# Row loads behind the inverse's blocks, and two scalings moved, in a chunked RWKV-7 and GELU kernel

## The chip, the cores and the metric

The kernel runs on one core of a Trainium2 chip. Its time is the device time of one execution in microseconds. TensorE (PE in the profile) multiplies matrices into PSUM, VectorE (DVE), ScalarE (ACT) and GpSimd (POOL) work on tiles in SBUF, and SyncE (SP) only issues transfers, one after the other in the order of the program. Engines run beside each other and wait for each other by semaphores. An instruction that waits holds up everything behind it on its own engine.

## The reference

```python
for t in range(S):                       # B, H, S, D = 4, 8, 768, 40
    y[:, :, t] = einsum('bhd,bhde->bhe', r_t, state)
    Sa = einsum('bhde,bhe->bhd', state, a_t)
    state = state * w_t[:, :, None, :] - einsum('bhd,bhe->bhde', Sa, b_t)
    state = state + einsum('bhd,bhe->bhde', v_t, k_t)
x = y.transpose(0, 2, 1, 3).reshape(B * S, H * D)    # 3072 x 320
h = x @ w_in                                          # 320 x 2048
out = (0.5 * h * (1 + erf(h / sqrt(2)))) @ w_out      # 2048 x 320
```

A recurrence over 768 tokens in 32 independent heads, then a two-layer network with an exact GELU. All arithmetic is in float32.

## The kernel before, in words

The sequence is cut into 12 chunks of 64 tokens (`NCH`). Within a chunk the recurrence is written as matrix products over the 64 tokens, with running products of w in the place of the step by step decay. The correction by a and b needs the inverse of a triangular 64x64 matrix for each head, built from `N`, the masked product of b and a.

That inverse goes a long way round. `make_N` (L571) masks the product on VectorE and has SP write its two diagonal 32x32 blocks to DRAM (four transfers, L586). `start_inverse` (L622) loads them back into `Nb`, with one block in each partition (two transfers, L635), and `columns()` (L639) eliminates the 31 columns on GpSimd: per column a product (L643) and a sum (L645). `store_inverse` (L651) writes the result to DRAM from GpSimd's queue (L657), and `fetch_inverse` (L660) brings it back as `Tt` and `T2` over SP's queue (six transfers, L667 and L671). `turn_corner` (L678) transposes a part of it into `L` on VectorE (L680), from which `corner` (J on TensorE) and `joined` (J2, then L710) make the off-diagonal block.

The main loop (L1121 to L1208) works on three chunks at once. In the pass of chunk c it finishes c (`corner`, `make_X`, `joined`, `make_sa`, `make_M`, `make_QY`, `outputs`), does the later preparation of n = c + 1 (`make_A`, `fetch_inverse`, `make_av`, `make_RV`, `turn_corner`) and begins n2 = c + 2: its loads, its sums of log w, its N and the start of its inverse. Between these steps `fill()` puts one portion of the network of an earlier chunk (`mlp`, and from the fourth chunk on `seven`, a form of the second layer with seven products in place of eight) on TensorE, so that it always has something to do. The order of the instructions on every engine is written out by hand: it is the order of the program.

For n2 several arrays are loaded. `load_next` brings w and a, `load_r`, `load_v` and two calls of `fetch_pairs` bring r, v, b and k in pairs of tokens for transposition (`a_pairs`, `r_pairs`, `v_pairs`, each tile used for two arrays in turn). Beside these, v, b and k are loaded once more as plain rows: `load_VR` (L197, tile `VR`) and `load_kb` (L193, tiles `b_rows` and `k_rows`, two of each in turn), six transfers of 160 KB. The rows of b and k are scaled by the inverse running product of w (`part`, written in `sums`, L425): b on VectorE in `scale_b` (L463), k on GpSimd in `scale_k` (L470). The scaled rows are first needed by `make_QY`, a pass later; the rows of v by `make_av`, in the next pass.

So SP's queue in one pass holds, in this order and beginning in the middle: w, a, r, b in pairs, v, k in pairs, the ten small transfers of `xt` (L802, L805, the input of the network), the rows of v, b, k, the six fetches of the inverse of n, the four of N of n2, the two of Nb of n2, and the four stores of an earlier chunk's output.

In `seven`, VectorE forms sums and differences of blocks of `gt`, the activated hidden layer: L868 makes a difference `s2`, L869 makes another in place in `block(1, 0)`, which the second product of the third group (`m7`) reads; L875 makes the one in `block(0, 1)` that the first product of that group reads.

Of the kernel before, what the change touches and what calls it, by code (L numbers as in the profile page):

```python
# [19 lines left out]
def kernel(  # L20
# [46 lines left out]
    nc = tc.nc  # L67
# [125 lines left out]
    def load_kb(c):  # L193
        fetch(c, "b", b, nc.sync)
        fetch(c, "k", k, nc.sync)

    def load_VR(c):  # L197
        VR = turned_in.setdefault(c, {})["VR"] = VR_ring()
        for e in range(2):
            nc.sync.dma_start(out=VR[half(e)].rearrange("p g q m d -> p (g q m) d")[:, :, :D], in_=rows_of(v, c, e))  # L200
# [195 lines left out]
    def run(steps):  # L396
        for _ in steps:
            pass
# [60 lines left out]
    def scale_b(c):  # L459
        rwv, wp = decays[c]  # L460
        nb = padded[:, c % 2] if c < NB else b_rows[c % 2]
        to = nb[:, :, :, :D] if c < NB else rows(nb)
        nc.vector.scalar_tensor_tensor(to, raws.pop((c, "b")), -1.0, rwv, ALU.mult, ALU.mult)  # L463
        turned_in[c]["nb"] = nb

    def scale_k(c, eng=nc.gpsimd):
        rwv, _ = decays.pop(c)
        ks = turned_in[c]["ks"] = padded[:, 2 + c % 2] if c < NB else k_rows[c % 2]
        to = ks[:, :, :, :D] if c < NB else rows(ks)
        eng.tensor_tensor(to, raws.pop((c, "k")), rwv, ALU.mult)  # L470

    def scale(c):
        scale_b(c)
        scale_k(c)
# [147 lines left out]
    def start_inverse(c, eng, place=None):  # L622

        n = P // 2
        blk = blocks.pop(c).rearrange("j z n s t -> (j z n) s t")
        if place is None:
            Nb = work.tile([P, BL * BL], FP32, tag="Nb", name="Nb")
            W = work.tile([P, BL // 2 * BL], FP32, tag="W", name="W")
            tmp = work.tile([P, BL * BL // 7], FP32, tag="tmp", name="tmp")
        else:  # L630
            Nb, W, tmp = place
        Nb, W = (t.rearrange("p (s t) -> p s t", t=BL) for t in (Nb, W))
        eng.memset(W, 0.0)
        for par in range(2):
            nc.sync.dma_start(out=Nb[par * n:(par + 1) * n], in_=blk)  # L635
            eng.memset(W[par * n:(par + 1) * n].rearrange("p s t -> p (s t)")[:, par::BL + 2][:, :BL // 2], 1.0)
        inverses[c] = W

        def columns():  # L639
            for j in range(BL - 1):  # L640
                rows, rest = j // 2 + 1, BL - 1 - j
                t = tmp[:, :rows * rest].rearrange("p (s t) -> p s t", s=rows)
                eng.tensor_tensor(t, W[:, :rows, j:j + 1].to_broadcast([P, rows, rest]),  # L643
                                  Nb[:, j:j + 1, j + 1:].to_broadcast([P, rows, rest]), ALU.mult)
                eng.tensor_tensor(W[:, :rows, j + 1:], W[:, :rows, j + 1:], t, ALU.add)  # L645
                yield
        return columns()
# [49 lines left out]
    def joined(c):  # L697
        t = turned_in[c]
        Tt, T2 = inverses.pop(c)
        Js = t.pop("Js")  # L700
        F = flat(Tt)
        J = duo("J2")[:, :, :G * NP * BL].rearrange("p z (n t) -> p z n t", n=G * NP)
        for n in range(2 * G * NP):
            for q in range(2):
                if n % 2:
                    mm(J[lo[q], 1, n // 2], Js[lo[q], n // 2], T2[lo[q], n // 2])
                else:
                    mm(J[lo[q], 0, n // 2], Js[hi[q], n // 2], F[hi[q], n, BL:])
        for q, copy in ((0, nc.scalar.copy), (1, nc.vector.tensor_copy)):
            copy(F[lo[q], :, BL:].rearrange("p (n z) t -> p z n t", z=2), J[lo[q]])  # L710
        t["Tt"] = Tt
# [115 lines left out]
    def block(g, z):  # L827
        return gt[:, z * NF // 2:(z + 1) * NF // 2, g * P:(g + 1) * P]
# [15 lines left out]
    def seven(c, s1, s2):  # L844
        t1, t2, t4 = sums_of_w
        t3 = quarter(0, 1)
        os = [work.tile([P, 2, DM // 2], FP32, tag="os", name="os", bufs=2) for g in range(G)]
        c11, c12, c21, c22 = os[0][:, 0], os[0][:, 1], os[1][:, 0], os[1][:, 1]

        def products_of(*factors):  # L850
            po = duo("po")
            for n, (l_, r_) in enumerate(factors):
                for f in range(NF // 2):
                    nc.tensor.matmul(po[:, n, :DM // 2], l_[:, f], r_[:, f], start=f == 0, stop=f == NF // 2 - 1)  # L854
            return po[:, 0, :DM // 2], po[:, 1, :DM // 2]

        def add(to, one_, other):
            nc.vector.tensor_tensor(to, one_, other, ALU.add)  # L858

        def store(g):  # L860
            for e in range(2):
                row = (G * e + g) * S + c * C
                nc.sync.dma_start(out=out[row:row + C], in_=os[g][half(e)].rearrange("p z d -> p (z d)"))

        m1, m2 = products_of((block(0, 0), quarter(0, 0)), (block(0, 1), quarter(1, 0)))
        if s2 is None:
            s2 = SM_ring().rearrange("p e g n c -> p (e g n c)")[:, :NF * P // 2].rearrange("p (f t) -> p f t", t=P)
            nc.vector.tensor_tensor(s2, s1, block(0, 0), ALU.subtract)  # L868
        nc.vector.tensor_tensor(block(1, 0), block(0, 0), block(1, 0), ALU.subtract)  # L869
        nc.scalar.copy(c12, m1)  # L870
        nc.scalar.copy(c11, m2)
        add(c11, c11, c12)
        yield
        m5, m6 = products_of((s1, t1), (s2, t2))
        nc.vector.tensor_tensor(block(0, 1), block(0, 1), s2, ALU.subtract)  # L875
        nc.scalar.copy(c22, m5)  # L876
        add(c12, c12, m6)
        yield
        m3, m7 = products_of((block(0, 1), quarter(1, 1)), (block(1, 0), t3))
        add(c21, c12, m7)  # L880
        add(c12, c12, c22)
        add(c12, c12, m3)
        add(c22, c22, c21)
        store(0)
        yield
        m4, _ = products_of((block(1, 1), t4))
        add(c21, c21, m4)
        store(1)
        yield
# [231 lines left out]
    for c in range(2, NCH):  # L1121
        n, n2 = c + 1, c + 2
        more, more2 = n < NCH, n2 < NCH
        corner(c)
        make_X(c)
        if c == NS + 1:
            weight_sums(3)
        if c == 2:

            seconds(1, (14, 14), last=True)  # L1130
            fill()
            turn_b(n)
            make_N(n)
            run(start_inverse(n, nc.gpsimd))
            store_inverse(n, (nc.gpsimd,))
            load_r(n)
            load_v(n)
        else:
            fill()
        if more2:  # L1140
            load_next(n2)
        joined(c)
        if c == 2:
            pieces.reverse()
            seconds(2, last=True)
        fill()
        make_sa(c)
        make_saT(c)
        if c == 2:
            turn_r(n)  # L1150
            scale_k(n, nc.vector)
            fill()
            pieces.reverse()
            fill(2)
            turn_k(n)
        if more2:
            load_r(n2)
        if more2:
            turn_a(n2)
            fetch_pairs(n2, "b_turned", b, nc.sync, False, paired["a"])  # L1160
        fill()
        make_y2(c)
        make_M(c)
        if more:
            turn_v(n)
        if more2:
            load_v(n2)
            turn_r(n2)
            fetch_pairs(n2, "k_turned", k, nc.sync, False, paired["r"])
        fill()  # L1170
        if more2:
            logs(n2)
        make_QY(c)
        outputs(c)
        pieces.append(mlp(c))
        fill()
        if c == NS:
            weight_sums(0)
            weight_sums(1)
        if more:  # L1180
            make_A(n)
        if more2:
            load_VR(n2)
            load_kb(n2)
            sums(n2)
        if more:
            turn_state()
            fetch_inverse(n)
            make_av(n)
        if more2:  # L1190
            scale_a(n2)
            turn_b(n2)
        fill()
        if c == NS:
            weight_sums(2)
        if more:
            make_RV(n)
        if more2:
            make_N(n2)
            scale(n2)  # L1200
            run(start_inverse(n2, nc.gpsimd))
            store_inverse(n2, (nc.gpsimd,))
        if more:
            turn_corner(n)
        fill()
        if more2:
            turn_k(n2)
        fill()  # L1208
# [31 lines left out]
```

## Time and profile before

| | |
|---|---|
| median of 13 runs | 729.3 us (724.92 to 732.57) |
| the profiled execution | 725.5 us, its span 723.8 us |
| TensorE busy, matmuls | 664.3 us (92%) |
| VectorE, GpSimd, ScalarE busy | 383.5, 349.0, 213.6 us |
| one chunk on TensorE, undisturbed | 50.7 us (337.18 to 387.91) |
| inverse on GpSimd, one chunk | 29.9 us (342.04 to 371.98) to 32.9 us (500.30 to 533.21) |
| DMA queue of SP | 52.4% of 16 engines |

The span runs from the first to the last instruction of the profiled execution, and its times count from there. A line of the timeline gives start, duration, engine, line and operation, the tile written and the tiles read, the count, and in brackets the idle time of the engine before it and what ended it. The chain that ended last is followed back from the last instruction, at each step to what released it. SPq and ACTq are the queues on which an engine issues transfers.

### The profile page before, as it was taken

Reading aid. Unit: us, or ns where it says so; the run is one execution under the profiler, and the core shown is the slowest. Engines: PE = TensorE matmul, PEld = TensorE weight load, DVE = VectorE, ACT = ScalarE, POOL = GpSimd, SP = SyncE. Lnnn points to the kernel's source line nnn. Section 1 sums busy time; section 2 is a strip of 40 time slices with the busy share of each in tenths; the row PEclk is TensorE's granted clock in tenths of the full one; section 3 lists DMA queues with packets and bytes.
Section 4 is the critical chain, followed back from the end, with each engine's and each line's share of the span. In section 5 each row is a group of like instructions: output and inputs, shape, how many; then the busy total and the mean of one; then the engine's idle time right before and its main releaser. Section 6 shows DMA issues by size and latency. Waiting matters only on the chain.

```text
span 723.8 us, 31335 instructions
## 1 busy us (share of the span) xinstructions
PE 664.3 (92%) x14096; PEld 583.0 (81%) x14096; DVE 383.5 (53%) x541; ACT 213.6 (30%) x279; POOL 349.0 (48%) x794
## 2 busy tenths in 40 slices
PE   7446789569999999999999999999999999999997
PEld 4345678557787887899899898998988998898987
DVE  2785569885255176275374473563753671621403
ACT  5115455343131240340341332232322323112020
POOL 4285248810661671862852853863863846800000
PEclk9655699779999999999999999999999999999999
DMA  9788738652766747657667567657556561020000
GB/s 119 130 166 151 139 89 208 144 109 68 146 127 103 141 85 137 107 100 129 116 114 132 98 115 133 114 93 131 116 94 129 105 112 50 22 53 3 25 14 19
DMA packets 284302, 75.75 MB, mean 105 GB/s; under 512 B 271976, under 2 KB 276872, under 8 KB 284168
## 3 DMA queue, kind: packets, MB, share of 16 engines
q1 hardware_dynamic: 283104, 71.22, 52.4%
q0 software_dynamic: 864, 2.36, 1.8%
q8 instruction: 111, 1.82, 1.1%
q14 instruction: 23, 0.19, 0.1%
q10 hardware_dynamic: 200, 0.16, 0.1%
HBM read 59.54 MB, written 10.22 MB: 96 GB/s over the span
## 4 chain that ended last, share of the span: by engine, by line
PE 62%; POOL 11%; DVE 7%; SPq 7%; DMA 6%; issue 4%; ACT 2%; ACTq 1%; DVEq 0%; POOLq 0%
PE ph L901 23%; PE po L854 11%; PE po L918 8%; POOL W L645 4%; PE QY L100 4%; POOL tmp L643 4%; PE cum L100 2%; PE J L100 2%; DMA N<-N 2%; PE X L100 2%; PE wT_ps L100 1%; DMA inv<-W 1%; PE RV_ps L100 1%; POOL st L645 1%; DMA Nb<-N 1%
## 5 line engine op out<-in xcount | busy, mean ns | idle before, releaser
L901 PE MATMUL ph<-xt,w_in_sb 64*128 64x256 f32 x1920 | 221.1, 383 | 0.5 <-ACT gt L903 0.4
L901 PEld LDWEIGHTS ph<-xt,w_in_sb 64*128 64x128 f32 x1920 | 183.4, 188 | 23.5 <-ACT gt L903 0.5
L643 POOL TENSOR_TENSOR tmp<-W,Nb 128x126 f32<-128x126 f32 (+22 forms) x310 | 127.6, 412 | 123.3 <-DMA Nb<-N 99.8
L645 POOL TENSOR_TENSOR W<-W,tmp 128x126 f32<-128x126 f32 (+22 forms) x310 | 132.3, 427 | 24.3
L903 ACT ACTIVATE gt<-ph 128x1024 f32<-128x1024 f32 x48 | 49.1, 1023 | 148.4 <-PE ph L901 124.3
L854 PE MATMUL po<-w_out_sb,gt 128*128 128x160 f32 x576 | 82.9, 302 | 0.1
L854 PEld LDWEIGHTS po<-w_out_sb,gt 128*128 128x128 f32 x576 | 78.7, 190 | 2.2 <-DVE gt L875 0.4
L918 PE MATMUL po<-w_out_sb,gt 128*128 128x320 f32 x192 | 55.4, 445 | 0.0
L918 PEld LDWEIGHTS po<-w_out_sb,gt 128*128 128x128 f32 x192 | 36.7, 195 | 15.5 <-issue 1.5
L470 POOL TENSOR_TENSOR k_rows<-k_rows,part 128x640 f32<-128x640 f32 x8 | 12.3, 1542 | 70.9 <-DMA k_rows<-in_k_dram 70.9
L549 DVE TENSOR_TENSOR SM<-M_ps,upper 128x1024 f32<-128x1024 f32 x12 | 14.7, 1223 | 45.9 <-PE M_ps L100 45.9
L710 DVE COPY Tt<-J 32x512 f32<-32x512 f32 x12 | 8.3, 689 | 55.4 <-ACT Tt L710 55.4
L694 ACT COPY Js<-J 128x256 f32<-128x256 f32 x12 | 4.4, 371 | 101.4 <-PE J L100 101.4
L906 DVE TENSOR_TENSOR half<-gt 128x1024 f32<-128x1024 f32 x9 | 11.7, 1305 | 38.6 <-ACT gt L903 38.6
L303 ACT ACTIVATE conv<-conv,rebias 128x320 uint32<-128x320 uint32 (+1 forms) x26 | 16.0, 624 | 35.1 <-DVE conv L302 34.8
L854 PE MATMUL po<-extra,half 128*128 128x160 f32 x176 | 26.1, 303 | 0.0
L858 DVE TENSOR_TENSOR os<-os,po 128x160 f32<-128x160 f32 x36 | 11.4, 316 | 25.9 <-ACT os L876 14.5
L738 DVE COPY SM<-sap 128x640 f32<-128x640 f32 x12 | 9.9, 824 | 28.2 <-PE sap L100 28.1
L903 ACT ACT_TABLE_LOAD x10 | 12.8, 1283 | 39.8 <-PE ph L901 39.8
L854 PEld LDWEIGHTS po<-extra,half 128*128 128x128 f32 x176 | 24.2, 190 | 0.3
L549 DVE TENSOR_TENSOR VR<-RV_ps,upper 128x1024 f32<-128x1024 f32 x12 | 14.7, 1223 | 17.5 <-PE RV_ps L100 17.5
L100 PE MATMUL av<-VR,A 64*64 64x40 f32 x768 | 15.2, 240 | 8.0 <-DVE A L549 8.0
(197 smaller groups left out, 1124.5 us busy)
## 6 DMA issues: line engine op xcount, KB each, us to landing
Nb<-N SPq DMA_DIRECT2D x22, 256.0 KB
VR<-in_v_dram SPq DMA_DIRECT2D x24, 160.0 KB
out_dram<-os SPq DMA_DIRECT2D x48, 80.0 KB
w_tile<-in_w_dram SPq DMA_DIRECT2D x22, 160.0 KB
b_rows<-in_b_dram SPq DMA_DIRECT2D x22, 160.0 KB
k_rows<-in_k_dram SPq DMA_DIRECT2D x22, 160.0 KB
w_out_sb<-in_moe_w_out_dram SPq DMA_DIRECT2D x11, 320.0 KB
N<-N SPq DMA_DIRECT2D x48, 64.0 KB
```

The costliest lines, as they stand in the source:

```text
L100: nc.tensor.matmul(o, lhsT, rhs, start=first, stop=True, skip_group_check=True)
L303: nc.scalar.activation(power, power, ACT.Relu, bias=rebias, scale=8.0)
L470: eng.tensor_tensor(to, raws.pop((c, "k")), rwv, ALU.mult)
L549: nc.vector.tensor_tensor(to, pt, upper.unsqueeze(1).to_broadcast([P, 2 * G * NP, C]), ALU.mult)
L643: eng.tensor_tensor(t, W[:, :rows, j:j + 1].to_broadcast([P, rows, rest]), Nb[:, j:j + 1, j + 1:].to_broadcast([P, rows, rest]), ALU.mult)
L645: eng.tensor_tensor(W[:, :rows, j + 1:], W[:, :rows, j + 1:], t, ALU.add)
L854: nc.tensor.matmul(po[:, n, :DM // 2], l_[:, f], r_[:, f], start=f == 0, stop=f == NF // 2 - 1)
L858: nc.vector.tensor_tensor(to, one_, other, ALU.add)
L901: nc.tensor.matmul(ph[:, x, s], w_in_sb[half(x), kt, p * P:(p + 1) * P], xt[half(x), kt], start=kt == 0, stop=kt == NK - 1)
L903: nc.scalar.activation(gt[:, 4 * q:4 * q + 4].rearrange("p (x s) t -> p x s t", x=2), ph, ACT.Gelu)
L906: nc.vector.tensor_tensor(s1, block(1, 0), block(1, 1), ALU.add)
L918: nc.tensor.matmul(po[:, g], gt[:, f, g * P:(g + 1) * P], w_out_sb[:, f], start=f == 0, stop=f == NF - 1)
```

## The change

Four edits, all in the passes of the main loop and in `seven`:

- The six loads of the rows of v, b and k for n2 leave their place ahead of `sums(n2)` and stand behind the start of the inverse of n2, that is behind N and Nb on SP's queue; b and k now go ahead of v.
- The scaling of b's rows leaves its place behind `make_N(n2)` and is done in the next pass, behind `joined`, for passes after that of chunk 2.
- The scaling of k's rows stays on GpSimd, but stands behind the first eight columns (`BL // 4`) of the inverse in place of ahead of it. `decays[c]` is read in place of popped, since the order of the two scalings is reversed.
- In `seven`, the difference in `block(1, 0)` is formed behind that in `block(0, 1)`, one portion later.

```diff
     def scale_k(c, eng=nc.gpsimd):
-        rwv, _ = decays.pop(c)
+        rwv, _ = decays[c]
...
             nc.vector.tensor_tensor(s2, s1, block(0, 0), ALU.subtract)
-        nc.vector.tensor_tensor(block(1, 0), block(0, 0), block(1, 0), ALU.subtract)
         nc.scalar.copy(c12, m1)
...
         nc.vector.tensor_tensor(block(0, 1), block(0, 1), s2, ALU.subtract)
+        nc.vector.tensor_tensor(block(1, 0), block(0, 0), block(1, 0), ALU.subtract)
         nc.scalar.copy(c22, m5)
...
         joined(c)
+        if c > 2 and more:
+            scale_b(n)
...
         if more2:
-            load_VR(n2)
-            load_kb(n2)
             sums(n2)
...
         if more2:
             make_N(n2)
-            scale(n2)
-            run(start_inverse(n2, nc.gpsimd))
+            steps = start_inverse(n2, nc.gpsimd)
+            load_kb(n2)
+            load_VR(n2)
+            for _ in range(BL // 4):
+                next(steps)
+            scale_k(n2)
+            run(steps)
             store_inverse(n2, (nc.gpsimd,))
```

## The prediction

> **What bounds the kernel now.** I read the page first, for the shares and the chain that ended last.
>
> ```profile
> PE 664.3 (92%) x14096; PEld 583.0 (81%) x14096; DVE 383.5 (53%) x541; ACT 213.6 (30%) x279; POOL 349.0 (48%) x794
> PE 62%; POOL 11%; DVE 7%; SPq 7%; DMA 6%; issue 4%; ACT 2%; ACTq 1%; DVEq 0%; POOLq 0%
> ```
>
> TensorE is the bound, yet a tenth of the chain is GpSimd. The chain in order of time says where: from 225 us to 411 us it is TensorE without a gap, from 415 us to 542 us it runs through SP's queue and two whole inverses on GpSimd, then TensorE again to the end. So a second loop takes over late. What that costs is the idle time of TensorE; the waits of that engine from 225 us on are these two:
>
> ```profile
> PE J L100 <- DVE L L680: 2.8, 2, 1.6
> PE av L100 <- DVE A L549: 0.8, 1, 0.8
> ```
>
> Next, TensorE's timeline around the first (corner products J; idle time before them in brackets):
>
> ```profile
> 438.02 0.74 PE L100 MATMUL J<-L,N 32*32 32x32 f32 x64
> 489.99 0.74 PE L100 MATMUL J<-L,N 32*32 32x32 f32 x64 [1.18 <-DVE L L680]
> 542.49 0.74 PE L100 MATMUL J<-L,N 32*32 32x32 f32 x64 [1.61 <-DVE L L680]
> ```
>
> and two pieces of the chain behind the last of these:
>
> ```profile
> 544.30 6.20 PE ph L901 x40
> 551.19 4.52 PE ph L901 x40
> ```
>
> After the 1.61 us gap one ph block took 6.20 us against 4.52 us, and the stretches show a granted clock of 0.77 and 0.70 there. So this gap cost 1.61 + 1.68 us. An undisturbed chunk takes 50.7 us (X at 337.18, next at 387.91); call T the start of a chunk's J.
>
> Now the loop that is late, in SP's timeline at the end of two chunks:
>
> ```profile
> 425.77 1.41 SPq L200 DMA_DIRECT2D VR<-in_v_dram  x2
> 427.23 2.56 SPq L153 DMA_DIRECT2D b_rows<-in_b_dram  x2
> 429.83 2.79 SPq L153 DMA_DIRECT2D k_rows<-in_k_dram  x2
> 433.05 3.12 SPq L667 DMA_DIRECT2D Tt<-inv  x4
> ...
> 486.62 1.92 SPq L667 DMA_DIRECT2D Tt<-inv  x4
> 489.67 3.09 SPq L586 DMA_DIRECT2D N<-N  x4
> 494.38 1.12 SPq L635 DMA_DIRECT2D Nb<-N  x2
> ```
>
> Six loads stand ahead of the fetch of the inverse and of N. N had been ready in VectorE since 432.73 (431.51 + 1.22), but went out at 437.29. Each chunk slips: GpSimd starts on Nb at 290.07, 342.04, 394.25, 447.44, 500.30, periods of 52.0, 52.2, 53.2 and 52.9 us against TensorE's 50.7. By the sixth the inverse ends so late that the fetch waits for it (486.62, 539.02), and TensorE waits for the fetch. GpSimd's 70.9 us of waiting for k_rows is no loss: it waits for Nb afterwards anyway (99.8 us).
>
> **What the Trainium skill says.** DMA: Bandwidth & Descriptors, "Issuing engines are not separate DMA queues": all DMAs end on the same 16 engines, so an order change moves their work and removes none. Agrees: one queue, 52.4% of 16 engines. Same page, "Queues, rings and completion order": descriptors of one ring are consumed in order[...]. No row of before tests that. GPSIMD Engine Reference, "Key points": GpSimd shares its SBUF interfaces with VectorE, and contends with VectorE instructions that have two SBUF inputs. Agrees: at 362.60 an update that takes 0.40 took 1.27 us, under half (L906); L868 and L869 did the same at 367.65 and 368.87, about 0.85 us each. TensorE: Matmul & The Clock Gate, "What's actually happening", gives one idle window of about 3.4 us before the clock halves; here a gap of 1.61 us was enough and one of 1.18 us was not. The trace decides.
>
> **The change part by part.**
>
> *Six loads behind Nb.* Removed ahead of the fetch: 1.41 + 2.56 + 2.79 = 6.8 us of SP issue (5.8 in the chunk at 337 us). SP is then through with xt at T+37 to 38 (373.7 in the chunk whose J is at 336.4) and waits for the inverse, no longer the inverse for SP. N is ready at T+45.6 (382.0), and goes out then: 5.1 us before the next T. From N's issue to Nb's 3.6 to 4.7 us (281.52 to 285.09; 489.67 to 494.38), and to GpSimd's start 5.1 (285.09 to 290.07 and its like), so GpSimd starts at T+3.6 to 4.7; before it was T+5 to T+10.
>
> The same 6 us now stand ahead of the out stores and the w, a, r and b_turned loads. From Nb to the end of a's issue took 7.3 us (495.59 to 502.85), so a's issue ends at about T+13 and it lands by T+17 (502.85 to 506.92: 4.1). Its turn on VectorE, wanted at T+14, waits to T+17; that has happened already (506.92, waited 3.4, T+16.9) without TensorE noticing, because the mask of M behind it is needed by QY at T+24.6 and takes 1.2: a may land as late as T+22. b_turned's issue waits for the turn; v's waits for vT at T+22.6 in both kernels, so SP has caught up there. r lands near T+24, wanted at T+22.5, and L906 behind it at T+25.5; w is wanted at T+26; VR a chunk later. The six loads' DMA work (three 2-us slices of 1.03, 1.09, 0.64: 5.5 us) falls into T+0 to T+18, where the slices sum to 12.7 of 18 us: full, not over. Cost nothing; without this cover a late a costs what exceeds T+22, 0 to 2 us a chunk.
>
> *k scaled within the inverse.* 1.54 us x 1 moves from GpSimd's idle time into the inverse, eight columns in (6.2 us: 342.04 to 348.2). So inverse, the inv store queued behind it on GpSimd, fetch and L are 1.54 us later from their start. Its wait for k: k is issued by T+3.5 and lands 4.1 us behind issue (379.65 to 383.76), at about T+8; it is asked for at T+10. Nothing; bound 0 to +2 us.
>
> *b behind the join.* 0.81 us leaves the place ahead of L and enters 2.77 us of idle time between L710 and L738. Cost 0. It has two SBUF inputs, so about 0.4 us for GpSimd. Ahead of L it gains nothing, as L waited for DMA.
>
> *L869 behind L875.* 1.22 us of VectorE leaves the place ahead of A's mask, and goes into the 1.13 + 0.48 us of idle time behind L875. It gains the 0.8 us that av waited in chunk 10, whose A came behind L868 and L869; elsewhere 0. Its collision moves out of most inverses: -0.85 us. Its consumer, the second product of m7, is some 2 us away: cost 0.
>
> *The new loop.* The inverse took 29.9 us where it ran early (342.04 to 371.98) and 32.9 late (500.30 to 533.21), where more of VectorE's two-input work falls into it. After: 29.9 + 1.54 + 0.4 - 0.85 = 31.0. It ends at T+35 to 36; to the fetch 5.8 to 6.5 (533.2 to 539.02, 480.1 to 486.62): T+42. Fetch 3.05: T+45, before N is ready at T+45.6. So N's issue is set by TensorE, and the slip is gone. L needs the fetch to begin by T+47.3 (3.4 us from 539.02 to J at 542.49): about 5 us to spare.
>
> *Sum.* 1.18 + 1.61 + 1.68 (clock) + 0.8 = 5.3 us. The profiled execution took 725.5 us (span 723.8), so 720.2 us. It lies 3.8 us below the median of 729.3. If the other runs lose the 3.8 elsewhere, 724.0; if it is more of the same waits, 720.2. I take 723.
>
> **The rivals.**
>
> *The inverse loop becomes the bound (slower).* With 1.54 us more in it the loop without any waits is inverse + 6.2 + 3.05 + 4.7 + 5.5 = inverse + 19.5 us; it exceeds 50.7 once the inverse is over 31.2 us, about where I put it. If it is 32.9 + 1.54 + 0.4 = 34.8, each chunk slips by 3.6; over 7 chunks 25 less some 6 of slack: up to 19 us, with a few clock dips; half of that is 739. For it: it was the late bound. Against: it starts 2 to 6 us sooner, and the long inverses are those that ran into L485, L494 and L875 (T+35 to T+41).
>
> *The gain is absorbed (same).* a, r or k come late by a few us and M's mask or the inverse hands on half a us a chunk: 8 x 0.6 = 5 us, 728 to 730. For it: the DMA work bunches behind Nb. Against: 5 us of slack in each.
>
> *More than the sum.* The median's 3.8 us is of the same kind, and gone: 719 to 720.
>
> **How the numbers follow.** Forecast (gain of 4 to 7, 721 to 727 us) 0.52; more than the sum 0.18; absorbed 0.13; slower by the loop 0.17. About 0.3% (2.2 us) is what a measurement can tell: faster 0.70, same 0.13, slower 0.17. The likeliest's own range is 720 to 727. The range leaves out 0.06 below 718 and the worse half of the slower case above 735, where a slip of 1 to 2 us a chunk still lies inside.
>
> **What would show it.** Right: SP waits at the fetch of the inverse in nearly every chunk, GpSimd starts on Nb at a steady period of 50.7 us, a short time after J; no wait of J for L, no clock dip near 542 us; av's 0.8 us gone; the turn of a waits 2 to 4 us in every chunk. Wrong: Nb to Nb over 50.7; J waiting for L in several chunks; QY waiting for M's mask; GpSimd waiting for k in mid inverse.

## The result, and the profile after

| | before | after |
|---|---|---|
| median | 730.1 us (48 runs, 723.2 to 736.1) | 724.0 us (11 runs, 719.6 to 727.0) |
| ratio after / before | | 0.9923, 95% interval 0.9892 to 0.9953 |
| profiled execution, span | 725.5 us, 723.8 us | 726.3 us, 724.6 us |
| X of chunk 3 to X of chunk 11 | 410.5 us | 406.5 us |

The change makes the kernel 6 us faster by the medians; 723 us was predicted. Ratios, here and below, leave out the runs that the record marks as slow, and so differ a little from the ratio of two medians. Yet its one profiled execution is no shorter than that of before. The reason lies ahead of everything that was changed: in the fourteen profiles of this case X of chunk 3 begins anywhere from 231.7 to 240.0 us, and already J of chunk 2, where neither kernel has executed a changed instruction, stands at 159.78 us in the profile before and at 164.32 us in that after. (J and X are the first two products on TensorE in the pass of a chunk, `corner` and `make_X`; T is the start of J, as in the prediction.) So spans of single profiles are not compared below. What is compared is the part from X of chunk 3 to X of chunk 11 (chunks counted from 0), and the periods between one X and the next.

The page after, its shares and the chain that ended last:

```profile
PE 662.2 (91%) x14096; PEld 580.2 (80%) x14096; DVE 386.6 (53%) x541; ACT 214.0 (30%) x279; POOL 340.4 (47%) x794
PE 78%; SPq 6%; DVE 6%; DMA 3%; POOL 3%; ACT 2%; issue 2%; ACTq 1%; DVEq 0%; POOLq 0%
```

GpSimd fell from 11% of the chain to 3%, and TensorE rose from 62% to 78%. The two waits of TensorE for another engine from 225 us on (waited for, in total, times, longest):

```profile
PE po L854 <- DVE gt L874: 0.3, 1, 0.3
PE av L100 <- DVE A L549: 0.3, 1, 0.3
```

The 2.8 us of J's waits are gone, and av's 0.8 us is 0.3; the 0.3 us of po lies behind X of chunk 11, in the network of the last chunks. SP's timeline around the corner products of chunk 6 (J at 392.30 us) shows the new order:

```profile
382.59 1.93 SPq L667 DMA_DIRECT2D Tt<-inv  x4
...
387.17 1.94 SPq L586 DMA_DIRECT2D N<-N  x4
390.64 1.67 SPq L635 DMA_DIRECT2D Nb<-N  x2
392.40 1.37 SPq L153 DMA_DIRECT2D b_rows<-in_b_dram  x2
393.82 2.32 SPq L153 DMA_DIRECT2D k_rows<-in_k_dram  x2
396.19 3.31 SPq L200 DMA_DIRECT2D VR<-in_v_dram  x2
```

The fetch goes out at T+41, N at T+45.6, Nb 1.7 us ahead of the next T, and the rows behind them. What ended SP's waits says who sets the pace now:

```profile
SPq L586 <- DVE N L549: 19.6, 8, 3.9
SPq L667 <- DMA inv<-W: 6.6, 5, 4.1
```

In all eight chunks N waits for its mask on VectorE, that is for TensorE. GpSimd's starts on Nb follow from it:

```profile
395.90 0.24 POOL L643 TENSOR_TENSOR tmp<-W,Nb 128x31 f32<-128x31 f32 x1 [12.39 <-DMA Nb<-N]
446.56 0.24 POOL L643 TENSOR_TENSOR tmp<-W,Nb 128x31 f32<-128x31 f32 x1 [13.86 <-DMA Nb<-N]
497.16 0.24 POOL L643 TENSOR_TENSOR tmp<-W,Nb 128x31 f32<-128x31 f32 x1 [13.67 <-DMA Nb<-N]
```

Periods of 50.7 and 50.6 us (and 50.6 to the next, at 547.71), where before had 52 to 53. The periods of TensorE, from one X to the next, worked out from the timelines of all kernels that are not far slower, show in which chunks the time was won:

```
us from X of chunk 3-4   4-5    5-6    6-7    7-8    8-9    9-10   10-11   sum
before          52.74  50.72  50.73  50.85  51.97  52.50  52.41  48.60   410.5
before_again    52.73  50.72  50.73  50.76  51.44  52.47  52.12  50.19   411.2
after           53.25  50.75  50.71  50.71  50.76  50.80  51.40  48.12   406.5
after_again     52.89  50.75  50.71  50.70  50.71  50.72  51.89  48.12   406.5
gt_back         52.74  50.76  50.71  50.71  50.71  50.71  52.03  48.63   407.0
gt_only         52.75  50.72  50.73  51.03  50.75  52.51  51.88  48.95   409.3
gt_only_again   52.76  50.72  50.73  50.73  50.89  50.91  50.73  48.11   405.6
rows_behind_a   53.06  51.03  51.02  51.03  51.07  51.06  51.78  48.12   408.2
loads_stay      52.74  50.72  50.73  51.76  53.73  52.69  53.88  50.93   417.2
kick            52.74  57.98  53.09  50.70  51.24  50.80  51.47  48.11   416.1
fill1           52.75  50.75  50.70  50.71  50.86  54.90  55.02  52.26   418.0
```

From chunk 4 to chunk 7 before and after are the same to 0.1 us. Before then loses 1.2, 1.7, 1.0 and 0.5 us in the last four periods against after, which gives 0.5 back in the first.

Two of these periods of after hold a loss that before does not have. TensorE's weight loads stop at these two places:

```profile
275.32 0.13 PEld L100 LDWEIGHTS av<-VR,A 64*64 64x64 f32 x1 [0.35 <-issue]
549.17 2.02 PEld L901 LDWEIGHTS ph<-xt,w_in_sb 64*128 64x128 f32 x19 [0.62 <-issue]
```

"issue" means that the profile shows nothing that was waited for. The first makes the 0.5 us of period 3-4, in after alone. The second stands in the middle of a ph block, the first layer of the network, behind J of chunk 9: period 9-10 of before lost 1.68 us to the slow clock, and after wins only 1.0 of it. The stop is there, 0.6 to 1.2 us long, in after, after_again, gt_back, rows_behind_a and kick, which all have the rows behind Nb and in which J of chunk 9 did not wait. In fill1, where that J waited, and in the five with the rows in their old place it is 0.15 us or nothing. Its cause stays open.

Repeats of both (before_again and after_again, kernels unchanged) give the same picture: 3.2 us of waits of J in three chunks there, none here; 722.5 us against 727.7, ratio 0.9944 (0.9917 to 0.9971). What was expected of after_again came true. In before_again the loop part is 0.7 us longer than in before, with one wait more, so a part of the spread between runs of before can be of this kind.

> The kernel before once more, for another profiled execution. If the 3.8 us by which its median lies above the first profiled execution are more of the same waits, J waits for L in more than two chunks and the loop part (from X at about 233 us to X of the eleventh chunk, 410.5 us in the first) is longer; if they are lost elsewhere, the loop part is the same and the time up to the first full pass differs.

> The full change once more, to set beside the two others of these runs: ratio 0.989 to 0.9955; J waits for L in no chunk, and from X of the third chunk to X of the eleventh 406 to 407 us, whatever the time before it.

### The profile page after: what moved, and what is told of

Its sections match the earlier page's. It is cut to its first block, busy times and chain, and to the rows that moved or that the text cites. A ratio compares the mean times of both kernels' runs of the same rounds, so it can differ in the third digit from the quotient of the medians.

```text
span 724.6 us, 31341 instructions
## 1 busy us (share of the span) xinstructions
PE 662.2 (91%) x14096; PEld 580.2 (80%) x14096; DVE 386.6 (53%) x541; ACT 214.0 (30%) x279; POOL 340.4 (47%) x794
## 4 chain that ended last, share of the span: by engine, by line
PE 78%; SPq 6%; DVE 6%; DMA 3%; POOL 3%; ACT 2%; issue 2%; ACTq 1%; DVEq 0%; POOLq 0%
PE ph L901 27%; PE po L854 18%; PE po L918 8%; PE QY L100 5%; PE J L100 2%; PE cum L100 2%; PE av L100 2%; PE RV_ps L100 2%; PE A_ps L100 2%; PE X L100 2%; PE wT_ps L100 1%; PE N_ps L100 1%; PE sap L100 1%; PE M_ps L100 1%; POOL st L645 1%
## 5 line engine op out<-in xcount | busy, mean ns | idle before, releaser
L643 POOL TENSOR_TENSOR tmp<-W,Nb 128x126 f32<-128x126 f32 (+22 forms) x310 | 124.5, 402 | 168.5 <-DMA Nb<-N 145.6
L645 POOL TENSOR_TENSOR W<-W,tmp 128x126 f32<-128x126 f32 (+22 forms) x310 | 126.6, 408 | 24.3
L918 PEld LDWEIGHTS po<-w_out_sb,gt 128*128 128x128 f32 x192 | 36.9, 195 | 15.6 <-issue 1.7
L176 DVE STREAM_TRANSPOSE aT<-a_pairs 128x1024 f32<-128x1024 f32 x9 | 11.2, 1246 | 31.7 <-DMA a_pairs<-in_a_dram 31.7
L100 PEld LDWEIGHTS av<-VR,A 64*64 64x64 f32 x768 | 14.1, 149 | 10.2 <-DVE A L549 8.5
```

Source lines behind the costliest of these rows:

```text
L100: nc.tensor.matmul(o, lhsT, rhs, start=first, stop=True, skip_group_check=True)
L176: nc.vector.transpose(to.rearrange("p n (s y) -> p n y s", y=2), raws.pop((c, n)).rearrange("p n (y d) -> p n y d", y=2)[:, :, :, :BL])
L918: nc.tensor.matmul(po[:, g], gt[:, f, g * P:(g + 1) * P], w_out_sb[:, f], start=f == 0, stop=f == NF - 1)
```

## The experiments

The theory: the late loop was N, Nb, inverse, fetch; taking the six loads out of it lets TensorE set N's time, and that is where the gain comes from. The rivals: the gain comes from another part (L869's move, which shortens the inverse; or b's scaling); and, for what the change risks, the longer inverse costs in proportion in place of staying hidden.

### loads_stay: the change without the move of the loads

```diff
         if more2:
+            load_VR(n2)
+            load_kb(n2)
             sums(n2)
...
             steps = start_inverse(n2, nc.gpsimd)
-            load_kb(n2)
-            load_VR(n2)
```

> The change with one part undone: the six loads of the rows of v, b and k back in their old place ahead of the fetch of the inverse; b and k are still scaled in their new places. My theory (the six loads ahead of the fetch make SP late by 6 us a chunk, until the inverse and TensorE wait): N leaves at T+48 again, GpSimd starts on Nb at T+5 and slips by 1 to 2.5 us a chunk, J waits for L in the last chunks, and the 1.54 us of k inside the inverse make it a little worse than before: 728 to 736 us, ratio to before 0.998 to 1.01. Rival (the gain comes from where b and k are scaled, no longer ahead of L and of the inverse): the time of the full change, ratio 0.99 to 0.995.

735.2 us against 728.9, ratio 1.0119 (1.0043 to 1.0195): slower than before, its time at the upper edge of what the theory gave and its ratio just above. SP at the end of chunk 6 (J of chunk 7 at 444.16, after a wait of 0.98 us):

```profile
430.85 1.41 SPq L200 DMA_DIRECT2D VR<-in_v_dram  x2
...
440.75 1.92 SPq L667 DMA_DIRECT2D Tt<-inv  x4
...
443.79 2.03 SPq L586 DMA_DIRECT2D N<-N  x4
449.02 1.13 SPq L635 DMA_DIRECT2D Nb<-N  x2
```

The six row loads hold SP from 430.85 to 437.4 us, and Nb goes out 4.9 us after J, where after has it 1.7 us ahead of J. By this chunk the loop is so late that the fetch, at 440.75, waits for the inverse itself. The loads show directly in the three chunks before it: there the fetch follows on the rows within 0.2 us, and N goes out at T+48.3 to 48.8, where after has T+45.6 to 46.0. J waits 7.5 us in five chunks. So the other three edits alone cost time, and the move of the loads, the only difference between this kernel and after, turns that into a gain. The likely reason for the cost is k's 1.54 us in a loop that is late already; no run takes the three edits apart here, and none moves b's scaling alone.

### k_ahead: the change, with k scaled ahead of the inverse's first column

```diff
             load_VR(n2)
-            for _ in range(BL // 4):
-                next(steps)
             scale_k(n2)
```

> The full change, but k scaled on GpSimd ahead of the first column in place of behind the eighth. k is issued behind Nb and lands about T+8.4, so GpSimd, which could start at T+3.3, starts at T+10. Theory: the loop N to Nb 3.5, Nb to k's landing 10, k 1.5, inverse 29.3, to the fetch 5.5, fetch 3.05 is 52.9 us against TensorE's 50.7; after one or two chunks J waits for L by about 2 us in each further one, with clock dips: 733 to 745 us, ratio 1.005 to 1.02. Rival (k's wait is hidden by slack of the loop, its place is free): ratio 0.99 to 0.995, no wait of J.

758.9 us against 728.9, ratio 1.0445 (1.0357 to 1.0533): the sign was expected, the size was not. GpSimd's waits and TensorE's:

```profile
POOL k_rows L470 <- DMA k_rows<-in_k_dram: 81.6, 5, 16.7
PE J L100 <- DVE L L680: 14.2, 6, 5.0
PE QY L100 <- DVE SM L549: 5.2, 3, 2.4
```

The inverse now starts when k has landed, not when Nb has: with Nb issued at 451.23 us the scaling began at 460.54 and the first column at 462.05, 10.8 us behind Nb's issue against 5.3 in after (390.64 to 395.90). TensorE's period becomes about 56 us; the 5.2 us of QY's waits were not in the expectation. So k must stand behind some columns once its load stands behind Nb: the two edits belong together.

### gt_back, gt_only, gt_only_again: L869 by itself

gt_back is the change with L869 in its old place; gt_only and gt_only_again are the kernel before with that move alone:

```diff
-        nc.vector.tensor_tensor(block(1, 0), block(0, 0), block(1, 0), ALU.subtract)
         nc.scalar.copy(c12, m1)
...
         nc.vector.tensor_tensor(block(0, 1), block(0, 1), s2, ALU.subtract)
+        nc.vector.tensor_tensor(block(1, 0), block(0, 0), block(1, 0), ALU.subtract)
```

> The full change without the moved difference of blocks in seven (it stands again behind L868). Theory: only one wait of av for A in chunk 10 returns (0.5 us more than with the change), and each inverse meets one more two-input instruction of VectorE (0.85 us), covered by 1.4 to 2.9 us of slack at N: within 0.2% of the full change, ratio 0.99 to 0.995. Rival (that move carries a share of the gain): ratio 0.995 or more.

> The kernel before with the moved difference of blocks in seven alone. Theory (it shortens each inverse by up to 0.85 us, but the six loads ahead of the fetch still set SP's pace, and av's wait of 0.8 us goes): GpSimd still starts on Nb at periods of 52 us, J waits late: 0 to 2 us faster than before, ratio 0.997 to 1.0. Rival (it carries a share of the gain): ratio 0.996 or less.

> The kernel before with L869 behind L875 alone, once more with more rounds. Theory: the move takes up to 0.85 us of collision out of each inverse, which holds the starts of GpSimd on Nb closer to TensorE's 50.7 us and saves most of the waits of J and the half-clock spell behind them: ratio 0.993 to 0.998; the nine corner products in the loop from the third chunk to the eleventh 407.5 to 409.5 us apart (before 410.5 and 411.2, the whole change 406.5); J waits under 3 us in all, no single wait above about 1.4 us; av's wait gone. Rival: the first measurement was luck, the move gives only av's 0.8 us: ratio 0.9985 or more, J waits as before.

| | time, before beside it | ratio (interval) | mean inverse of eight | J waits in the profile |
|---|---|---|---|---|
| gt_back | 724.4, 728.9 us | 0.9949 (0.9922 to 0.9976) | 32.4 us | none |
| gt_only | 724.2, 727.7 us | 0.994 (0.9912 to 0.9969) | 30.8 us | 3.0 us in 3 |
| gt_only_again | 725.2, 725.1 us | 1.0001 (0.9974 to 1.0028) | 30.4 us | none |
| before, before_again | | | 31.3, 31.8 us | 2.8 in 2, 3.2 in 3 |
| after | | | 31.6 us | none |

The inverse is measured from GpSimd's start on Nb to its store; that of after and gt_back holds k's 1.54 us. The change without L869's move keeps a gain in the same bounds as the whole change, so the move isn't what the gain rests on, and the theory stands there. (By its ratio alone gt_back lies on the border of what theory and rival gave; its part from chunk 3 to chunk 11, 407.0 us, 0.5 us above after, and J without a wait decide.) But the move does what its step said to the inverse: 0.8 us shorter in after than in gt_back, and 0.5 to 1.4 us shorter in the kernel before. In that kernel this can be enough to keep the loop on time: in the profile of gt_only_again GpSimd starts at 243.15, 294.36, 347.11, 399.10, 449.56, 500.26, 553.16 and 601.99 us, 51.3 us apart on average against 51.9 before, J never waits, and the part from chunk 3 to chunk 11 takes 405.6 us.

The two measurements do not agree, though: one gave 0.994 and the other 1.0001, with intervals that do not even touch. The kernel with the move differs by 1.0 us between them, the kernel before by 2.6 us; over all sets of runs before has medians from 725.1 to 730.1 us, and what makes it faster in some was not found. (The profile of gt_only is of a run of 731.8 us, near the top of its range of 718.7 to 732.4, so its waits say less than its times.) What the move is worth by itself in the kernel before stays open, within 0.9912 and 1.0028. It cannot simply be added to the gain of the rest, since gt_back without it has nearly all of the change's gain: both act on one slip, and where that is gone there is little left to save. So the move of the loads is enough for the gain, but it isn't shown to be the only way to it.

### fill4, fill2, fill1, kick: how much room is left

These lengthen the inverse of the change by GpSimd operations that add and subtract the same array, so the output is the same to rounding: four and two of 1.54 us in each inverse (fill4, fill2), two half as large (fill1, 1.8 to 2.4 us together), and eight in one single inverse (kick). The edit of fill4 is shown; fill2 has `range(2)`, kick `range(8 if c == 3 else 0)`, and fill1 `range(2)` on half of the columns.

```diff
             scale_k(n2)
+            ks, rw = rows(turned_in[n2]["ks"]), decays[n2][0]
+            for m in range(4):
+                nc.gpsimd.tensor_tensor(ks, ks, rw, ALU.subtract if m % 2 else ALU.add)
             run(steps)
```

> The full change with four more GpSimd instructions of k's size (add and subtract of the same array, 4 x 1.54 = 6.2 us) behind the scaling of k, inside the inverse. Theory (loop of inverse, store, fetch, N, Nb with 1.4 to 2.9 us of slack at N and 6 to 7 at J): the loop is 54.5 us, it slips 3.7 us a chunk from the second on, J waits for L in five to seven chunks, with clock dips: 745 to 762 us, ratio 1.02 to 1.045. Rival (the loop has no hold on the end any more, TensorE alone sets it): the time of the full change.

> The full change with two more GpSimd instructions of k's size (an add and its subtraction, 3.1 us) behind the scaling of k. Theory of the switch: beyond the slack by about 1 us at the first late chunk; then the loop feeds on itself and J waits in the last two to four chunks: 735 to 752 us, ratio 1.008 to 1.032. Rival (in proportion): 3.1 us cost 27, 751 us, ratio 1.03 and J late from the third or fourth chunk on, by the same amount in each.

> The full change with two more GpSimd instructions of half k's size (an add and its subtraction, together some 1.6 us) behind the scaling of k. With the change the fetch of the inverse begins at T+39.5 to T+41 and could begin as late as T+42.4 before N leaves late. Theory (one switch: as long as the added time is below the slack of 1.4 to 2.9 us at N, TensorE sets the pace; beyond it the loop runs late, and grows by itself, since a late inverse meets more of VectorE's two-input instructions, 33.5 us against 29.3 without k, and N to Nb takes 5.0 in place of 3.5 us): at the edge, 722 to 728 us, ratio 0.99 to 1.0, no more than a few us of waits of J. Rival (the price is in proportion to the added time: four instructions of 6.2 us cost 55 us, so 1.6 us cost 14): 738 us, ratio 1.012.

> The full change with one delay: eight GpSimd instructions of k's size (12.3 us) inside the inverse of the sixth chunk, begun in the pass of the fourth, and none in the others. Theory of two states (late, the loop takes 53 to 54 us by itself, as in the run with the loads in their old place, and TensorE's 50.7 can't catch up): J waits for L in the next pass by some 5 us, and goes on waiting in all later ones, with a period of 53 to 54 us of GpSimd's starts on Nb to the end: 740 to 752 us, ratio 1.018 to 1.032. Rival (a delay is paid once, the loop without it falls back to its place): one wait of 5 to 7 us and a clock dip, then starts of GpSimd 50.7 us apart: 728 to 733 us, ratio 1.0 to 1.008.

| | added to one inverse | ratio (interval) | inverse, late chunks | period late |
|---|---|---|---|---|
| fill1 | 1.8 us (late chunks) | 1.0218 (1.0156 to 1.028) | 35.1 to 36.9 us | 55.0 us |
| fill2 | 3.1 us | 1.0263 (1.0193 to 1.0333) | 38.2 us | 55 to 56 us |
| fill4 | 6.4 us | 1.0718 (1.0644 to 1.0792) | 41.4 us | 58 to 60 us |
| kick | 13.4 us, once | 1.0117 (1.0057 to 1.0178) | 32.3 us | 50.7 to 51.5 us |

fill1 and fill4 came out above everything that was expected of them. fill2 came out within both its theory and, with its interval, its rival, and J waited in six chunks and not in the last two to four: it decides nothing between them. Why the price is so high can be read in the inverses: 3.1 us more made the inverse not 34.5 but 38.2 us long. GpSimd in fill2, in the pass of the chunk whose J began at 448.78 us, four operations late in the inverse (start, duration):

```profile
486.43 1.23 POOL L643 TENSOR_TENSOR tmp<-W,Nb 128x96 f32<-128x96 f32 x1
489.50 1.39 POOL L645 TENSOR_TENSOR W<-W,tmp 128x78 f32<-128x78 f32 x1
490.98 1.20 POOL L643 TENSOR_TENSOR tmp<-W,Nb 128x70 f32<-128x70 f32 x1
492.26 1.19 POOL L645 TENSOR_TENSOR W<-W,tmp 128x70 f32<-128x70 f32 x1
```

and VectorE in the same microseconds:

```profile
485.96 1.48 DVE L485 TENSOR_TENSOR aT<-aT,wpT 128x1024 f32<-128x1024 f32 x1 [0.77 <-ACT wpT L419]
489.47 1.23 DVE L494 SCALAR_TENSOR_TENSOR nT<-nT,en 128x1024 f32<-128x1024 f32 x1
490.62 1.36 DVE L874 TENSOR_TENSOR gt<-gt,SM 128x1024 f32<-128x1024 f32 x1
491.90 1.36 DVE L875 TENSOR_TENSOR gt<-gt 128x1024 f32<-128x1024 f32 x1
```

Each of four VectorE operations with two inputs in SBUF holds up one GpSimd operation, which takes 1.2 to 1.4 us where its kind takes 0.4 on average (page of before), some 0.85 us each and 3.4 us together. It is the collision of which the Trainium skill speaks (GPSIMD Engine Reference, "Key points": shared interfaces to SBUF), with its price here. In after the same four begin at T+35.4, 38.9, 40.1 and 41.2, and the inverse ends just short of them (J at 392.30 us):

```profile
427.26 1.63 POOL L657 DMA_DIRECT2D inv<-W  x2 [0.30 <-POOL W L645]
427.70 1.22 DVE L485 TENSOR_TENSOR aT<-aT,wpT 128x1024 f32<-128x1024 f32 x1 [0.77 <-ACT wpT L419]
```

So the length of the inverse depends on when it runs. Ending at T+35 it takes 31.4 us; pushed later it meets L485 and then the others, and each makes it later still. fill1 shows the edge: its inverses of 34.0 to 34.8 us (31.4 us and the 2.3 us that the added operations took there make 33.7, so most of one such collision more) kept pace for four chunks, and J began at 342.25, 393.00 and 443.71 us without a wait. Then it tipped:

```profile
494.57 0.74 PE L100 MATMUL J<-L,N 32*32 32x32 f32 x64
549.47 0.74 PE L100 MATMUL J<-L,N 32*32 32x32 f32 x64 [2.08 <-DVE L L680]
```

The next two waits are 2.30 and 2.31 us. What seems to have set it off stands in SP's queue: N issued straight behind a late fetch took 3.09 us to issue, and Nb went out 4.8 us behind it (438.89 to 443.66) against 3.5 in the chunks before; the inverse that followed took 35.8 us.

kick asks whether a late loop recovers. Two states were expected to be kept by themselves, with a loss in every later chunk; that fell. The time, 735.9 us, lies between what theory and rival gave. J waited once, and the clock fell once behind it (granted clock 0.78 from 350 to 360 us, and a period of 53.09 us for 50.7); the next J's waited for nothing. TensorE's timeline, J of two chunks:

```profile
348.33 1.08 PE L100 MATMUL J<-L,N 32*32 32x32 f32 x64 [6.88 <-DVE L L680]
401.75 0.75 PE L100 MATMUL J<-L,N 32*32 32x32 f32 x64
```

The loss adds up: 6.9 us of waiting, 2.3 us of the slow clock (53.09 less 50.75) and 0.5 us in one later chunk make the 9.6 us by which kick's part from chunk 3 to chunk 11 exceeds after's. GpSimd's starts on Nb, at 357.25, 408.47, 459.39, 509.51, 559.86 and 610.29 us, tell how the loop came back. They stand 8.9, 6.7, 6.9, 5.8, 5.4 and 4.3 us behind J, and their periods are 51.2, 50.9, 50.1, 50.35 and 50.4 us. A pressed loop of the change, with an inverse of 32.3 us, thus runs at 50.1 to 51.2 us, about as fast as TensorE and no faster. The change has room in time (its fetch begins at T+39.5 to 41.6 from chunk 5 on and could begin at T+47.3 by the prediction's reckoning, so 6 us or more at J) but hardly any in rate (about half a us a chunk).

### rows_behind_a: the rows one step later still

The change leaves a's load behind the six row loads, so a's turn waits. This kernel issues the rows behind w and a of the next pass, and scales k behind 16 columns:

```diff
             steps = start_inverse(n2, nc.gpsimd)
-            load_kb(n2)
-            load_VR(n2)
-            for _ in range(BL // 4):
+            for _ in range(BL // 2):
                 next(steps)
-            scale_k(n2)
-            run(steps)
-            store_inverse(n2, (nc.gpsimd,))
```

and, in the next pass behind `load_next(n2)`, `load_kb(n)`, `load_VR(n)`, `scale_k(n)`, the rest of the inverse and its store.

> The full change with the six row loads one step later still: behind the loads of w and a of the next pass; k is scaled behind 16 columns of the inverse in place of 8. It takes the price away that I put at nothing: the turn of a on VectorE, which with the change waits for its load until T+19 in place of T+14 to T+17. Theory (that wait is covered by idle time of VectorE up to T+22): the turn of a starts by T+16 again, VectorE's 30 us of waiting for a go down to under 10, and the time is that of the full change within 0.3%, ratio 0.989 to 0.9955. Rival (the lateness of a is passed on in small gaps of TensorE): 2 to 4 us faster than the full change.

725.6 us against 727.1, ratio 0.9985 (0.9958 to 1.0012): neither as fast as the change nor faster, so both expectations missed. The 30.4 us of the turn's waiting for a (seven waits) are gone, as meant, and bought nothing; in after, too, none of TensorE's stops stands at them. TensorE has no wait for J, but its period is 51.0 to 51.1 us in place of 50.7 to 50.8 in the five periods from chunk 4 to chunk 9. TensorE's weight loads for M_ps in one chunk of this kernel (QY's began at 412.51), and in after (QY's at 410.37):

```profile
413.77 1.02 PEld L100 LDWEIGHTS M_ps<-rT,saT 40*64 40x64 f32 x64 [0.23 <-ACT gt L903]
```

```profile
411.30 1.03 PEld L100 LDWEIGHTS M_ps<-rT,saT 40*64 40x64 f32 x64
```

M_ps starts 1.26 us behind QY in place of 0.93, and waits for ScalarE's GELU in seven chunks. That is the 0.32 us of the period; over the part from chunk 3 to chunk 11 the kernel takes 1.7 us more than after. The ratios put it some 3 to 4 us behind the change, so a part of that is not accounted for. Why the GELU comes into M_ps's way in this order was not settled.

## Why the prediction was right, step by step

- **The slip and what it cost.** Right. N goes out when VectorE has it, in all eight chunks, at T+45.6 as predicted or up to 0.7 us later; loads_stay shows that the place of the loads decides it. The waits of J and the slow spell of the clock near 542 us went with it, and the spell's price of 1.68 us was right. But the prediction set the gap that was enough (1.61 us) beside the one that was not (1.18 us), as if the length decided; the last section shows that it does not, so how many spells a run loses could not be read from its gaps.
- **GpSimd's start at T+3.6 to 4.7.** T+3.1 to 4.0 from chunk 5 on. The rows behind Nb do not hold it up: from Nb's issue to GpSimd's start it takes 4.7 to 5.3 us in after, 4.6 to 5.9 in before. The fetch at T+42: T+39.5 to 41.6 from chunk 5 on. It waits for the inverse in five chunks of eight, not in nearly all, as the sign named for it had it.
- **a's late turn.** The turn waits in seven chunks, 30.4 us in all, and TensorE doesn't notice: right. From chunk 5 on it begins at T+18.0 to 19.2 and not at T+17 (410.93 with J at 392.30), so some 3 us are left to the T+22 named as its limit, not 5, and the waits are 2.8 to 5.5 us long, not 2 to 4. rows_behind_a removes the wait without any gain.
- **k inside the inverse.** No wait for k, 1.54 us of work: right. The need for the columns ahead of it is shown by k_ahead.
- **b behind the join.** It fits its gap (L738 still waits 0.82 us behind it), but in most chunks the collision goes the other way than written: not GpSimd's operation is held up, but VectorE's takes up to 1.92 us in place of 0.82. Cost nothing, as predicted.
- **L869.** av's wait fell from 0.8 to 0.3 us, so 0.5 of its 0.8 us was gained; the 0.85 us of collision per inverse came out at 0.8 (gt_back to after).
- **The new inverse, 31.0 us.** 31.3 to 31.7 us in the third to the seventh of the eight, 29.8 in the first, 32.6 in the second and 33.3 in the last. The constant around it, put at 19.5 us for a loop without waits, is 17.8 to 19.2 us by kick's periods less its inverses. The two errors offset each other, and that was luck: with 19.5 us and 31.4 us the rival "the inverse loop becomes the bound" would have come true, slightly. The prediction gave it less than one chance in five on the ground that the inverse would run ahead of L485, L494 and L875, and this is what the fill kernels show to be decisive.
- **The sum.** 5.3 us were to be gained in the profiled execution. The last four periods gained 4.4 us, the first gave 0.5 back: 4.0 us, and 4.7 us between the two repeats. Of the difference 0.3 us is av's, 0.5 us the stop of the first period and 0.6 to 0.7 us that of chunk 9: the waits and the clock were gained as reckoned, and the two stops, which the prediction did not have, take a part back. That the median gained more (6.1 us, and 5.3 us in the repeat) than the profile would fit the remark that the median run of before loses more than its profiled one: the runs of before reach 736.1 us, those of after end at 727.0, while the fastest are alike (719.0 us in all runs of before, 719.6 of after; there are fewer runs of after, so the ends of the ranges say little by themselves). The profiles only show single runs, so that the rest of before's spread is also made of waits of J was not seen directly.

## What to carry to other kernels

A load that nobody needs for a pass should not stand, on an in-order queue, ahead of a small transfer that closes a loop between engines: here 6.8 us of issue made a loop 1.3 to 2.5 us slower than the bound, and it took five chunks to be felt. Before lengthening a step of such a loop, ask two things: how late it may be, and how fast the loop runs when it is late; the change has 6 us of the first and half a us of the second, and 1.8 us more tips it. And ask what stands just behind a step on the engine beside it: a step that ends short of its neighbour's two-input work grows when it is pushed into it.

## What the hardware showed beyond expectation

- A collision on SBUF is paid by whichever of the two begins second. Where VectorE's L463 met GpSimd's own two-input L470 behind its start, it took 1.92 us for 0.82, and L470 kept its 1.54; where L463 began first, it kept its 0.83 us, and L470 took 2.13. From the timeline after:

```profile
401.94 1.54 POOL L470 TENSOR_TENSOR k_rows<-k_rows,part 128x640 f32<-128x640 f32 x1
402.25 1.92 DVE L463 SCALAR_TENSOR_TENSOR b_rows<-b_rows,part 128x640 f32<-128x640 f32 x1
...
605.92 0.83 DVE L463 SCALAR_TENSOR_TENSOR b_rows<-b_rows,part 128x640 f32<-128x640 f32 x1
606.01 2.13 POOL L470 TENSOR_TENSOR k_rows<-k_rows,part 128x640 f32<-128x640 f32 x1
```

  The four collisions of fill2 are of the second kind: VectorE begins 0.03 to 0.5 us ahead, and GpSimd's operation ends 0.2 us behind VectorE's. So a short operation pays what is left of the long one that it meets.
- The length of a gap on TensorE does not decide whether the clock falls behind it. In loads_stay J waited 0.98 us at 444.16 us, and the granted clock was 0.58 from 446 to 450 us; it waited 1.26 us at 497.89 and 1.41 us at 604.45, and the clock stayed at 1.00 behind both (498 to 510 and 605 to 640 us). A spell as in before, at half clock from about 544.5 to 548 us, costs 1.7 us.
- The work ahead of the changed passes, the same in all kernels, ends 8 us apart from one profile to another (J of chunk 2 begins at 158.0 to 165.7 us); nothing in the kernels tells why, and the granted clock up to there does not either (0.77 in before, 0.81 in after, which is the later). It is larger than what was to be measured, which takes many runs, or a part of the profile in place of its span.
